# Spreading filter rows by DMA from SBUF to SBUF in an FFT-filter and max-out kernel

## Chip, cores, metric

One core of one Trainium2 chip. The metric is the device time of one execution in microseconds (us), the median of the runs of one session. All runs compared here are in the fast state or, where there was only one run, of unknown state; no slow run is used. Ratios are the mean time of one kernel's runs over the mean time of the other's in the same rounds, so not quite the ratio of the medians that are quoted.

## The reference

```python
X = np.fft.rfft(x, axis=1)                    # x: 8 x 3072 x 256
Y = X * (filt_r + 1j * filt_i)[None]          # filter: 1537 x 256
y = np.fft.irfft(Y, n=3072, axis=1).reshape(24576, 256)
out = np.maximum(y @ w1, y @ w2) @ w_out      # w1, w2: 256 x 1024; w_out: 1024 x 256
```

## The kernel before

Each batch goes through four transform stages: S1 (matrix C1, result `at`, written to HBM as `ad`, read back as `bt`), S2 (matrix U, result `px`; VectorE multiplies it by the filter rows F to `pq`), S3 (matrices VP and VQ, result `zt`, written as `zd`, read back as `zr`) and S4 (G1, result `y`). Then come 48 tiles of the second half: `ph` = y against w1 - w2, a relu to `gt`, and `po` = gt against w_out. A tile has eight steps of about 1 us, and the transform of the next batches is planned into these steps. Batch 0 goes through a special *opening* before the first `ph`.

F must hold the filter rows in a spread order of partitions (groups of 12 rows, every eighth source row). TensorE makes it with selection matrices from `Fs`, which has the rows as they lie in HBM, and ScalarE or VectorE evict the result:

```python
    def expand_f(g, ri, E, sp=0):
        ...
        for b in range(2):
            for c in range(2):
                m = 4 * b + c
                TE.matmul(pf[b][64 * c:64 * c + 32], Sel[:, m], fs[:, 2 * g:2 * g + 2], start=True, stop=True)
                ...                                   # and the mirrored rows, 32 partitions on
        evac(E, f_, p_...)                            # to F[:, ri, :, 2 * g:2 * g + 2]
```

The opening in the order of its program (cut); `first_s2` makes px and pq of one group g of rows:

```python
    V.memset(F0[:, :, :, 0:1], 0.0)
    load_f0()                       # 12 small DMAs on SyncE
    patch_f0()                      # 2 more, into rows that one of the 12 wrote
    first_s1(5, S, 2)
    expand_f(6, 0, V)
    ...
    expand_f(1, 1, S)
    expand_f(7, 0, S)
    pend = []
    for n, g in enumerate((1, 2, 3, 4, 5, 0, 6, 7)):
        pend.append(first_s2(g, n in (0, 1, 2, 4, 6)))
        if n < 6:
            first_t1(order[n + 2], V)
        ...
        if n < 6:
            expand_f((0, 3, 4, 5, 6, 7)[n], 1, S)
        ...
        if n > 1:
            first_s3(*pend.pop(0))
```

The plan of the first batches:

```python
    plan(6, f1_read, 1)                               # bt of batch 1
    plan_f2(1, spaced(17, 1.9, 9), 28, 34)            # S2/S3 of batch 1; zr in halves at 28 and 34
    plan_x(2, (5, 7, 8, 10, 11, 13), 6)               # load and fold x of batch 2
    plan(36, f1_read, 2)
    plan_x(3, spaced(24, 3, 6))
```

## Time and profile before

| | before |
|---|---|
| time, median of 2 | 527.7 us (527.67 to 527.74) |
| span in the profile | 523.8 us |
| TensorE busy | 504.0 us (96%) |
| pq of step n=3 starts | 29.92 us |
| last pq of the opening ends | 43.94 us |
| first `ph` starts | 48.24 us |
| from there to the end | 475.6 us |

The span splits at the first `ph`: ahead of it other engines pace TensorE, after it TensorE is nearly dense. The profiled execution took 525.53 us, some 2 us less than the median.

### The profile page before, as it was taken

How to read it: one execution, taken by the hardware profiler on the slowest of the kernel's cores; microseconds unless marked ns; L12 is line 12 of the kernel's file. 1: busy time of each engine (PE TensorE's matmuls, PEld its weight loads, DVE VectorE, ACT ScalarE, POOL GpSimd, SP SyncE). 2: the span in 40 equal slices, each digit the busy share in tenths (PEclk: the TensorE clock that was granted, in tenths of full speed). 3: DMA queues.
4: the chain of work that ended last, by engine and by line, in shares of the span. 5: the costliest groups of instructions: out<-in, count | busy, mean ns of one | idle time of the engine just before them, and what ended most of it. 6: DMA issues, size and time to landing. Idle time of an engine off the chain costs nothing.

```text
span 523.8 us, 12526 instructions
## 1 busy us (share of the span) xinstructions
PE 504.0 (96%) x5204; PEld 346.5 (66%) x5282; DVE 322.4 (62%) x437; ACT 336.9 (64%) x597; POOL 148.0 (28%) x168
## 2 busy tenths in 40 slices
PE   8988989999999999999999999999999999999997
PEld 3556655666667766676666666676667666677775
DVE  8986567435773476437783588537783588544432
ACT  6786658746885588756675577647675556645542
POOL 6683118264027204530066002720000000000000
PEclk9999999999999999999999999999999999999999
DMA  7990699997798969796798769894467936341212
GB/s 143 280 204 23 176 199 320 334 204 177 232 247 241 208 195 300 229 200 185 219 266 201 182 179 241 266 202 139 143 172 157 176 111 150 100 125 41 82 62 100
DMA packets 74093, 97.03 MB, mean 185 GB/s; under 512 B 5106, under 2 KB 49780, under 8 KB 73044
## 3 DMA queue, kind: packets, MB, share of 16 engines
q1 hardware_dynamic: 63012, 63.72, 52.6%
q0 software_dynamic: 11024, 32.51, 20.1%
q8 instruction: 41, 0.67, 0.6%
q14 instruction: 16, 0.13, 0.1%
HBM read 54.79 MB, written 47.19 MB: 195 GB/s over the span
## 4 chain that ended last, share of the span: by engine, by line
PE 76%; issue 1%; DVE 1%; ACT 0%
PE po L621 30%; PE ph L596 26%; PE po L616 7%; PE pz L447 4%; PE py L580 3%; PE px L469 2%; PE pa L410 2%; DVE pq L474 0%; ACT at L413 0%; DVE ot L623 0%
## 5 line engine op out<-in xcount | busy, mean ns | idle before, releaser
L601 ACT ACTIVATE gt<-ph 128x512 bf16<-128x512 f32 x308 | 182.1, 603 | 125.5 <-PE ph L596 124.0
L621 PE MATMUL po<-Wo,gt 128*128 128x256 bf16 x1536 | 229.8, 273 | 3.4
L621 PEld LDWEIGHTS <-gt 128*128 128x128 bf16 x1536 | 150.2, 98 | 57.6
L474 DVE TENSOR_TENSOR pq<-px,F 120x1024 bf16<-120x1024 f32 x112 | 131.7, 1219 | 32.6 <-PE px L469 32.4
L623 DVE COPY ot<-po 128x512 f32<-128x512 f32 x96 | 66.2, 690 | 103.9 <-PE po L621 102.3
L628 POOL DMA_DIRECT2D out_dram<-ot x47 | 25.8, 548 | 311.0 <-DVE ot L623 298.8
L402 POOL TENSOR_TENSOR xd<-xf 128x512 bf16<-128x512 f32 x72 | 89.1, 1268 | 47.2 <-DMA xf<-in_x_dram 46.2
L596 PEld LDWEIGHTS <-Wd 128*128 128x128 bf16 x768 | 70.8, 98 | 21.2 <-issue 12.6
L451 ACT ACTIVATE zt<-pz 112x512 bf16<-112x512 f32 x112 | 61.0, 602 | 19.5 <-PE pz L447 16.4
L599 DVE TENSOR_SCALAR gt<-ph 128x512 bf16<-128x512 f32 x76 | 52.2, 687 | 29.4 <-PE ph L596 22.0
L413 ACT ACTIVATE at<-pa 128x512 bf16<-128x512 f32 x72 | 39.2, 596 | 15.6 <-PE pa L410 15.4
L580 PE MATMUL py<-G,zr 128*128 128x128 bf16 x384 | 30.1, 219 | 1.9 <-ACT zr L514 0.7
L447 PE MATMUL pz<-pq,VP 56*64 56x256 bf16 x448 | 29.4, 271 | 1.1 <-DVE pq L474 0.8
L580 PEld LDWEIGHTS <-zr 128*128 128x128 bf16 x384 | 25.3, 98 | 5.1 <-issue 3.6
L447 PE MATMUL pz<-pq,VQ 56*64 56x256 bf16 x448 | 28.6, 268 | 0.0
L469 PE MATMUL px<-bt,U 48*64 48x256 bf16 x448 | 23.5, 274 | 1.0 <-DMA bt<-ad 1.0
L469 PEld LDWEIGHTS <-U 48*64 48x64 bf16 x448 | 11.6, 106 | 9.2 <-issue 6.0
L447 PEld LDWEIGHTS <-VP 56*64 56x64 bf16 x448 | 14.1, 105 | 3.7 <-issue 2.4
L530 DVE TENSOR_TENSOR pq<-px,F 120x1024 bf16<-120x1024 f32 x11 | 13.2, 1222 | 3.5 <-ACT F L514 1.9
L410 PE MATMUL pa<-xd,C 64*64 64x512 bf16 x144 | 15.2, 400 | 0.0
L514 ACT ACTIVATE F<-pf 128x1024 bf16<-128x1024 f32 x10 | 10.1, 1032 | 6.7 <-PE pf L134 6.7
L447 PEld LDWEIGHTS <-VQ 56*64 56x64 bf16 x448 | 13.9, 106 | 0.0
(387 smaller groups left out, 591.2 us busy)
## 6 DMA issues: line engine op xcount, KB each, us to landing
out_dram<-ot POOLq DMA_DIRECT2D x47, 512.0 KB, 5.1
xf<-in_x_dram SPq DMA_DIRECT2D x72, 256.0 KB
ad<-at SPq DMA_DIRECT2D x42, 256.0 KB
bt<-ad SPq DMA_DIRECT2D x56, 192.0 KB
zd<-zt SPq DMA_DIRECT2D x56, 192.0 KB
zr<-zd SPq DMA_DIRECT2D x14, 768.0 KB
xb<-in_x_dram POOLq DMA_DIRECT2D x12, 256.0 KB, 10.6
wf<-in_moe_w_dram POOLq DMA_DIRECT2D x2, 1024.0 KB, 10.3
```

The lines of the kernel that those rows point to most:

```text
L402: G.tensor_tensor(xb[b, c][:, i], xf[:, 0], xf[:, 1], op)
L413: S.activation(at[:, 2 * m:2 * m + 2], pa[m], AF.Copy)
L447: TE.matmul(pz[c][64 * k:64 * k + 64, i], W[64 * c:64 * c + 56, 2 * g + i, k], pq[k][64 * c:64 * c + 56, ri, i], start=(ri == 0), stop=(ri ...
L451: S.activation(zt[0:ROWS, c, o:o + 2], pz[c][0:ROWS], AF.Copy)
L469: TE.matmul(px[k][64 * c:64 * c + 64, i], U[64 * k:64 * k + 48, 4 * g + 2 * i + c], bt_[64 * k:64 * k + 48, t_], start=True, stop=True)
L474: V.tensor_tensor(pq[k][0:FROWS], px[k][0:FROWS].rearrange("p (o i) d -> p o i d", o=1).to_broadcast([FROWS, 2, 2, D]), F[0:FROWS, :, k, 2 ...
L580: TE.matmul(py[:, n], zr[b][:, 4 * i + n, 128 * dc:128 * dc + 128], G1, start=True, stop=True)
L596: TE.matmul(ph, Wd[:, dc, 128 * j:128 * j + 128], y_[:, dc].rearrange("p a b -> p (a b)"), start=(dc == 0), stop=(dc == 1))
L599: V.tensor_scalar(gt[tt][:, j], ph, 0.0, None, OP.max)
L601: S.activation(gt[tt][:, j], ph, AF.Relu)
L621: TE.matmul(p_, g_[:, jj, 128 * n:128 * n + 128], Wo[:, jj], start=False, stop=(jj == 7))
L623: V.tensor_copy(ot[tt][:, n - 1:n + 1], po[tt])
```

## The change

The intent: take evictions off ScalarE and products off TensorE in the opening by letting the idle SyncE queue spread the later filter rows (groups 6 and 7 of the real half, 4 to 7 of the imaginary half) by 32 DMAs from Fs to F; move x loads of batch 2 into the time where the DMA engines are idle; give S2/S3 of batch 1 twenty steps instead of seventeen. The core of the diff:

```diff
+    def spread_f(ri, g0):
+        n = 16 - 2 * g0
+        for b in range(2):
+            for c in range(2):
+                m = 4 * b + c
+                for q in range(2):
+                    p0 = 64 * c + 12 * q
+                    nc.sync.dma_start(out=F[p0:p0 + J, ri, b, 2 * g0:16], in_=Fs[ri][m:m + 89:8, 2 * g0:16])
+                    nc.sync.dma_start(out=F[p0 + 32:p0 + 32 + J, ri, b, 2 * g0:16],
+                                      in_=Fs[ri][7 - m:96 - m:8, n:0:-1])
 ...
+    clear_f(0, 6, G)            # zeros under the copied rows, on GpSimd
 ...
+    clear_f(1, 4, S)            # and on ScalarE
 ...
-    expand_f(6, 0, V)
+    expand_f(1, 1, S)
     first_t1(1, V)
     first_t1(2, V)
-    expand_f(1, 1, S)
-    expand_f(7, 0, S)
+    spread_f(1, 4)
+    spread_f(0, 6)
+    expand_f(2, 1, S)
 ...
-            first_t1(order[n + 2], V)
+            first_t1(order[n + 2], (V, S)[n > 2])
 ...                             # 4 expansions less in the loop, Wd(0) from GpSimd to VectorE at n=3
+    f1(1, 0, S)                 # S1 of batch 1: four parts in the tail of the opening
+    f1(1, 1, V)
+    for c in (3, 4, 5):
+        load_p(2, c)            # half of x of batch 2
 ...
-    s4(0)
-    f1(1, 0, V)
-    f1(1, 1, S)
+    first_s4()                  # S4 of tile 0 in halves
+    f1(1, 2, V)
+    f1(1, 3, S)
 ...
-    plan(6, f1_read, 1)
-    plan_f2(1, spaced(17, 1.9, 9), 28, 34)
-    plan_x(2, (5, 7, 8, 10, 11, 13), 6)
+    plan(5, f1_read, 1)
+    plan_f2(1, spaced(15, 2.4, 9), 28, 36)
+    for c in range(3):
+        plan(6 + c, load_p, 2, c)
+        plan(7 + 2 * c, fold_x, 2, 3 + c)
+        plan(15 + 2 * c, fold_x, 2, c)
```

More of the change, by code (lines that the diff above doesn't have):

```diff
@@ L143, in expand_f, with clear_f @@
             evac(E, f_, p_.rearrange("p b u d -> p b (u d)"))
+    def spread_f(ri, g0):
[8 more added lines that the diff above has]
+                                      in_=Fs[ri][7 - m:96 - m:8, n:0:-1])
+    def clear_f(ri, g0, E):
+        f_ = F[:, ri, :, 2 * g0:16].rearrange("p b u d -> p b (u d)").bitcast(FP32)
+        if E is S:
+            S.activation(f_, zero.rearrange("p (a b) -> p a b", a=1).to_broadcast([128, 2, (16 - 2 * g0) * D // 2]), AF.Copy)
+        else:
+            E.memset(f_, 0.0)
     F0 = zpool.tile([64, 2, 2, D], FP32, tag="zt", name="F0")
@@ L338, in spin, with prep_wd @@
             TE.matmul(pd, Sp, Sp.rearrange("p (o x) -> p o x", o=1).to_broadcast([128, 4, 128]), start=True, stop=True)
-    def prep_wd(k, w1f, w2f):
-        G.tensor_tensor(Wd[:, k], w1f[:, k], w2f[:, k], OP.subtract)
+    def prep_wd(k, E, w1f, w2f):
+        E.tensor_tensor(Wd[:, k], w1f[:, k], w2f[:, k], OP.subtract)
     def load_wo():
@@ L386, in load_p @@
     def load_p(b, c):
-        if c == 0:
+        if b not in big and c < 3:
             big[b] = late.tile([128, 3, 2, 2 * D], FP32, tag="l0", name="xf")
@@ L404, in f1_half @@
     def f1_half(b, c):
-        if c == 0:
+        if b not in ad:
             ad[b] = dram.tile([128, N2, D], BF16, tag="ad", name="ad")
@@ L463, in gen_f2 @@
             if b + 1 < B and j in units:
-                f1_half(b + 1, units.index(j))
+                f1_half(b + 1, (3, 4, 5, 0, 1, 2)[units.index(j)] if b == 1 else units.index(j))
             px = [ps.tile([128, 2, D], FP32, tag="ps", name="px") for _ in range(2)]
@@ L586, in s4, with first_s4 @@
         yt[tt] = y_
+    def first_s4():
+        y_ = ypool.tile([128, 2, 4, 128], BF16, tag="yt")
+        for h in range(2):
+            for dc in range(2):
+                py = ps.tile([128, 2, 128], FP32, tag="ps", name="py")
+                for n in range(2):
+                    TE.matmul(py[:, n], zr[0][:, 2 * h + n, 128 * dc:128 * dc + 128], G1, start=True, stop=True)
+                o = y_[:, dc, 2 * h:2 * h + 2]
+                if dc == 0:
+                    S.activation(o, py, AF.Copy, scale=1.0 / 1536.0)
+                else:
+                    V.tensor_scalar(o, py, 1.0 / 1536.0, None, OP.mult)
+        yt[0] = y_
     gt = {}
@@ L683 @@
         if n < 6:
-            first_t1(order[n + 2], V)
+            first_t1(order[n + 2], (V, S)[n > 2])
         if n == 0:
             tables_pe()
-            expand_f(2, 1, S)
-        if n < 6:
-            expand_f((0, 3, 4, 5, 6, 7)[n], 1, S)
+        if n < 2:
+            expand_f((3, 0)[n], 1, S)
         if n < 2:
@@ L693 @@
             fix_f()
-        if n in (1, 3):
-            tables_q(n // 2, S)
-        if n in (4, 6):
-            prep_wd(n // 2 - 2, *wf)
+        if n in (1, 2):
+            tables_q(n - 1, S)
+        if n == 3:
+            prep_wd(0, V, *wf)
+        if n == 6:
+            prep_wd(1, G, *wf)
         if n in (4, 5):
@@ L748 @@
         plan(j - 1, first_t2, j, V)
-    for c in range(2, 12):
-        plan(int(0.6 * (c - 1)), f1, 1, c, (S, V)[c % 2])
-    plan(6, f1_read, 1)
-    plan_f2(1, spaced(17, 1.9, 9), 28, 34)
-    plan_x(2, (5, 7, 8, 10, 11, 13), 6)
+    for c in range(4, 12):
+        plan(int(0.6 * (c - 3)), f1, 1, c, (S, V)[c % 2])
+    plan(5, f1_read, 1)
[4 more added lines that the diff above has]
+        plan(15 + 2 * c, fold_x, 2, c)
     plan(36, f1_read, 2)
@@ L771, in in_f2 @@
     def in_f2(step):
-        return 0 <= step < 6 or 17 <= step < 35 or 60 <= step < 82 or 104 <= step < 130
+        return 0 <= step < 6 or 15 <= step < 36 or 60 <= step < 82 or 104 <= step < 130
     for tt in range(6 * B + 1):
```

## The prediction

> **What bounds the kernel now.** I read the page first, then the busy time by stretches, then the opening's timelines of VectorE and of the SyncE queue, then the DMA view of short stretches.
>
> ```profile
> PE 504.0 (96%) x5204; PEld 346.5 (66%) x5282; DVE 322.4 (62%) x437; ACT 336.9 (64%) x597; POOL 148.0 (28%) x168
> ...
> DMA  7990699997798969796798769894467936341212
> ...
> PE 76%; issue 1%; DVE 1%; ACT 0%
> ```
>
> TensorE sets the time: it is busy 96% of the span and is nearly the whole of the chain that ended last. No change of evictions or loads can help where it is already dense, so I looked for the stretches where it isn't (columns: PE, PEld, DVE, ACT, POOL busy, PE clock, DMA share, GB/s).
>
> ```profile
> 0.00:48.24 48.24, 41.79 (x678) 24.29 (x682) 40.05 (x95) 35.70 (x53) 33.46 (x49) 1.00 0.83 171
> 48.24:116.00 67.76, 63.68 (x617) 42.89 (x626) 40.22 (x50) 45.52 (x84) 27.46 (x25) 1.00 0.93 237
> 116.00:500.00 384.00, 378.56 (x3757) 264.44 (x3819) 234.25 (x283) 247.91 (x448) 85.52 (x91) 1.00 0.72 184
> ```
>
> 48.24 us is where the first product of the second half (ph) starts. From 116 us on TensorE lacks 5.4 us of 384, all of it outside the change. From 48 to 116 us it lacks 4.1 us. The opening is the rest: 41.79 us busy there include 7.16 us of the 25 idle-filling matmuls at the start, so it is held by chains through the other engines. In its second half VectorE paces it:
>
> ```profile
> 29.92 2.36 DVE L530 TENSOR_TENSOR pq<-px,F 120x1024 bf16<-120x1024 f32 x2 [0.51 <-ACT F L514]
> ...
> 33.40 1.22 DVE L530 TENSOR_TENSOR pq<-px,F 120x1024 bf16<-120x1024 f32 x1 [0.53 <-ACT VQ L514]
> ...
> 41.58 2.36 DVE L530 TENSOR_TENSOR pq<-px,F 120x1024 bf16<-120x1024 f32 x2 [0.70 <-issue]
> ```
>
> These multiply S2's result by the filter rows F. Step n=3 (rows g=4) starts at 29.92 us, the last step ends at 43.94, and the first ph follows 4.3 us later. VectorE waits about half a us per step for ScalarE's copies of F, VQ and the like.
>
> **Where the DMA stands.** The new copies go out on SyncE behind the small loads of F0, so their present timing matters most:
>
> ```profile
> 18.59 2.31 SPq L154 DMA_DIRECT2D F<-in_filt_r_dram  x6
> 20.94 5.21 SPq L154 DMA_DIRECT2D F<-in_filt_i_dram  x6
> 27.77 0.24 SPq L157 DMA_DIRECT2D F<-in_filt_i_dram  x1
> 28.06 0.25 SPq L158 DMA_DIRECT2D F<-in_filt_r_dram  x1
> ```
>
> The first eight leave one after the other (298 to 435 ns each); the ninth leaves only at 23.85 us, and the wait view names the landing of a filter-row DMA. Nine waits for one: this program keeps eight of a queue in flight. The first one needed 23.85 - 18.59 = 5.3 us to land, the second patch (the fourteenth DMA) leaves at 28.06. The DMA views of 18 to 22 us and of 22 to 26 us show why:
>
> ```profile
> q0 software_dynamic: 513, 1.27, 104.8%
> ```
>
> ```profile
> q0 software_dynamic: 339, 1.20, 91.8%
> q1 hardware_dynamic: 205, 0.15, 13.3%
> ```
>
> In the first stretch SyncE's queue (q1) got not one packet; in the second about as many per engine as the GpSimd loads (q0). Those loads fill the engines until about 39 us.
>
> [...]
>
> **The change, part by part.**
>
> *Six expansions fewer.* Of 16 expansions of F (8 matmuls, about 0.44 us of TensorE each, and an eviction) groups 6 and 7 of the real and 4 to 7 of the imaginary half go. TensorE saves 6 x 0.44 = 2.6 us, ScalarE 5 evictions of 0.92 us pitch = 4.6 us, VectorE two of 0.6 = 1.2 us. Added: a clear of 2048 elements on ScalarE, by the like clear of At (1.89 us), which fits in its idle 2.17 us before 9.78; one on GpSimd, at most some 1 us (a guess), ahead of load issues that wait for landings anyway (1.8 us before the one at 9.36). Both cost nothing on the path.
>
> *Work moved to balance.* Three copies of bt (0.6 us pitch on VectorE, 1.0 on ScalarE) go to ScalarE at n=3 to 5, and half of Wd (2.34 us on GpSimd, as a tensor product of 1024 elements like pq some 1.15 on VectorE) to VectorE. VectorE gains 0.6 us, ScalarE 1.6.
>
> *32 copies from SBUF to SBUF.* Half move 12 rows as 12 long pieces, half as 12 x 8 (or 12 x 4) pieces of 512 B. The first 16 (imaginary, g 4 to 7) are 16 x 12 x 4 KB = 0.79 MB, the other 16 half that. They follow the patch at 28.06 us. Issue alone at 0.35 us: 28.4 + 16 x 0.35 = 34; plus some 2 us to land, **36 us** is the earliest for the row groups that n=3 needs at 29.92. With eight in flight, a landing of 3 to 5 us in the full queue and turns with q0 it is more. Per engine a 4 KB piece of q0 at the 209 GB/s of 30 to 38 us takes 4 KB / (209/16) = 0.31 us; the copies, from the 47 ns that a 490 B packet took in 64 to 68 us, about 0.4 us for eight small pieces and 0.15 for a long one (estimates). Eight pairs: 8 x (2 x 0.31 + 0.55) = 9.4 us, with start and landing 28.4 + 9.4 + 2 = **40 us**. I choose **38**.
>
> From there VectorE has left: eight pq (two at n=3, 5 and 7, one at n=4 and 6, where GpSimd makes the other) at a pitch of 1.15 us (two took 2.36) = 9.2, Wd 1.15, two w2T copies 1.2: 11.55 us. The end of pq goes to 38 + 11.6 = 49.6, against 43.94: **+5.6 us**. GpSimd and ScalarE work in parallel below that. The second 16 copies are needed some 7 us after the first and should be there.
>
> *End of the opening.* Four parts of batch 1's S1 run in TensorE's gaps of 44 to 48 us instead of one before the first ph: 3 x 0.22 = 0.65 us; S4 split in halves shortens the chain by perhaps 0.3: **-0.9 us**.
>
> *First batches.* Between 67 and 72 us S2 of batch 1 waits 0.37 + 0.64 us for bt and 0.84 us for VectorE; at 89 to 91 us 0.22 and 0.64 more, at 113 us 0.46; some slow matmuls beside these. Half of x of batch 2 now comes in the idle 39 to 48 us, bt is read before the other half, and 20 steps instead of 17 ease VectorE and ScalarE. Of 4.1 us I take **-2.8**.
>
> Sum: 527.7 + 5.6 - 0.9 - 2.8 = **529.6**, rounded to 529.5 us.
>
> **Rivals.** *(A) The copies come in time*: then ScalarE's freed 4.6 - 3.0 - 0 = 1.6 us and VectorE's 0.6 shorten steps 3 to 7 by 2 to 3 us, and the time is 527.7 - 2.5 - 0.9 - 2.8 = 521.5. For it: somebody tuned which groups are copied and moved work from exactly those steps. Against: the queue's 28.06 us. *(B) Full turns with the GpSimd loads*, and each small piece taking its own turn: first group at 44 us, opening +11.6, time 527.7 + 11.6 - 3.7 = 535.6; [...] *(C) The loop doesn't gain*, because bt's reads of 512 B pieces are what is late (about 160 GB/s in 64 to 72 us), not the x loads beside them: then 529.6 + 2 = 531.5.
>
> **Range and chances.** A and B bound the likely outcomes: 521 to 536. To be over 2% faster needs 10.6 us; all idle of the first batches and 6 us of opening together hardly give it: 0.03. Over 2% slower needs first groups after 47 us: 0.04. The rest, 0.93, lies within 2%; inside it I hold faster and slower about even, leaning to slower.
>
> **What would show it.** In the changed profile: the first spread copy leaves SyncE at about 28.4 us and the sixteenth between 34 and 38; VectorE's pq of n=3 waits for a DMA of F, not for ScalarE, and starts at 36 to 41 us instead of 29.9; first ph near 53 us; PEclk may dip in the third to fourth slice. From the first ph to the end the time is 2 to 4 us shorter, with no wait of px for bt. Wrong if pq of n=3 starts before 33 us (then the copies left earlier or landed in about 2 us), or if some later wait for F's second copies, or for xb, ends the opening.

## The result, and the profile after

548.5 us (547.16 and 549.84) against 527.7: ratio 1.0394, 95% interval 1.0285 to 1.0503. The change is slower by 3.9%, outside the predicted range.

The page of the changed kernel, TensorE's clock in 40 slices and the chain that ended last by engine:

```profile
PEclk9985789998999999999999999999999999999999
...
PE 79%; DMA 9%; SPq 4%; DVE 4%; ACT 1%; issue 1%; POOL 0%; POOLq 0%; DVEq 0%; ACTq 0%
```

Before, the clock row was 9 throughout and the chain had neither DMA nor SPq, the queue that SyncE issues from. Now the end hangs on 9% of DMA and 4% of *issuing*. The SyncE queue's timeline after (start, duration, line; L152 and L153 are the two copies of `spread_f`):

```profile
29.31 0.24 SPq L175 DMA_DIRECT2D F<-in_filt_i_dram  x1
29.59 0.25 SPq L176 DMA_DIRECT2D F<-in_filt_r_dram  x1
30.02 0.86 SPq L152 DMA_DIRECT2D F<-Fs  x1
30.99 0.88 SPq L153 DMA_DIRECT2D F<-Fs  x1
...
36.02 0.82 SPq L153 DMA_DIRECT2D F<-Fs  x1
...
44.25 0.82 SPq L153 DMA_DIRECT2D F<-Fs  x1
...
57.73 0.82 SPq L153 DMA_DIRECT2D F<-Fs  x1
```

The first copy leaves at 30.02 us, the eighth at 36.02, the sixteenth at 44.25, the last at 57.73. One copy takes 0.74 to 0.96 us to issue, where the F0 loads of the same profile took 0.27 to 0.44. Two of the copies (the twelfth and the fourteenth) also waited up to 1.0 us until an earlier one had landed: the fourteenth left at 42.60, when the sixth had (34.38 + 8.21 us). While the second sixteen go out, the DMA engines have almost nothing to do. The DMA view of 46 to 58 us has for SyncE's queue (packets, MB, share of the 16 engines' time):

```profile
q1 hardware_dynamic: 602, 0.35, 11.2%
```

VectorE's products pq in the opening after, which answer to those at 29.92, 33.40 and 41.58 us before:

```profile
43.42 1.22 DVE L549 TENSOR_TENSOR pq<-px,F 120x1024 bf16<-120x1024 f32 x1 [12.46 <-DMA F<-Fs]
47.12 1.22 DVE L549 TENSOR_TENSOR pq<-px,F 120x1024 bf16<-120x1024 f32 x1 [2.48 <-DMA F<-Fs]
...
60.22 1.23 DVE L549 TENSOR_TENSOR pq<-px,F 120x1024 bf16<-120x1024 f32 x1 [0.50 <-PE pz L567]
```

Step n=3 waits 12.46 us for its first product (rows b=0, in the first eight copies) and 2.48 for its second (b=1, the next eight). The last products can't start before the last copy, whose issue ended at 58.55 and which landed at 59.9 us; for VectorE's last one the timeline names only the wait that it took to be the last, one for TensorE, but the chain that ended last runs through the copies (four of its pieces: start, duration, what):

```profile
34.38 8.21 DMA F<-Fs
...
57.73 2.17 DMA F<-Fs
...
60.24 2.13 POOL pq L549
...
62.42 0.52 PE pz L567 x28
```

The piece of 8.21 us is the sixth copy, from its issue to its landing. The last product on this chain isn't VectorE's but GpSimd's, for step n=6 (rows b=1): it had waited 10.8 us for the copies and ended at 62.4 us, while GpSimd's last product before had ended at 42.2, ahead of VectorE's. The first `ph` starts at 67.93 us.

TensorE's clock was granted at 0.54 between 46 and 58.6 us and at 0.82 from there to 67.93 (0.50 in each whole microsecond from 65 to 71): the matmuls that prepare the first tile run partly at half speed. At tile 6 the clock fell after a wait of 4.36 us (below). In the opening it fell between 37 and 38 us (1.00 in the microsecond before, 0.50 in the one after), though TensorE had been busy for 1.94 us of 33 to 37 us, by matmuls whose ends the profile models. It fell again between 64 and 65 (1.00 before, 0.50 after), where its longest pause in the 4 us before was 1.79 us (until 62.42). What makes the clock fall isn't shown.

The second loss is at tile 6, whose S4 needs zr of batch 1. TensorE's timeline after:

```profile
127.90 0.59 PE L629 MATMUL ph<-y__2011,Wd 128*128 128x512 bf16 x2
...
133.40 1.01 PE L599 MATMUL py<-G,zr 128*128 128x128 bf16 x8 [4.36 <-DMA zr<-zd]
134.67 1.11 PE L629 MATMUL ph<-y__2144,Wd 128*128 128x512 bf16 x2 [0.26 <-ACT y__2144 L602]
```

A wait of 4.36 us for zr, and then ph takes 1.11 us instead of 0.59: the clock has dropped again (0.98 from 127 to 133 us, 0.50 from 133 to 139).

| | before | after | difference |
|---|---|---|---|
| pq of n=3 starts | 29.92 | 43.42 | +13.5 |
| from there to the end of the last pq | 14.0 | 18.0 | +4.0 |
| from there to the first ph | 4.3 | 6.5 | +2.2 |
| from there to the end | 475.6 | 479.9 | +4.3 |
| span | 523.8 | 547.8 | +24.0 |

Here "last pq" is VectorE's. The profiled executions took 525.53 and 549.84 us, one faster and one slower than its kernel's median, so the 24.0 us are 3.2 more than the 20.8 between the medians; in which rows these lie isn't known.

### The profile page after: what moved, and what is told of

Same layout as the page of the kernel before. It is cut to its first block, busy times and chain, and to the rows that moved or that the text cites.

```text
span 547.8 us, 12572 instructions
## 1 busy us (share of the span) xinstructions
PE 513.6 (94%) x5234; PEld 350.0 (64%) x5234; DVE 323.5 (59%) x434; ACT 337.1 (62%) x597; POOL 146.5 (27%) x168
## 4 chain that ended last, share of the span: by engine, by line
PE 79%; DMA 9%; SPq 4%; DVE 4%; ACT 1%; issue 1%; POOL 0%; POOLq 0%; DVEq 0%; ACTq 0%
PE ph L629 30%; PE po L654 29%; PE po L649 7%; PE pz L466 4%; PE py L599 3%; DMA zd<-zt 3%; PE px L488 3%; PE pa L429 2%; DMA F<-Fs 2%; SPq L152 2%; SPq L153 2%; DMA zr<-zd 1%; DMA F<-in_filt_i_dram 1%; DVE F L141 1%; DMA ad<-at 1%
## 5 line engine op out<-in xcount | busy, mean ns | idle before, releaser
L488 PE MATMUL px<-bt,U 48*64 48x256 bf16 x448 | 22.6, 274 | 0.5 <-DMA bt<-ad 0.5
L549 POOL TENSOR_TENSOR pq<-xs,F 120x1024 bf16<-120x1024 f32 x5 | 10.7, 2137 | 23.9 <-ACT M L533 11.0
L540 PE MATMUL px<-bt,U 48*64 48x256 bf16 x64 | 4.5, 313 | 10.2 <-DVE pq L549 10.0
```

The costliest lines, as they stand in the source:

```text
L488: TE.matmul(px[k][64 * c:64 * c + 64, i], U[64 * k:64 * k + 48, 4 * g + 2 * i + c], bt_[64 * k:64 * k + 48, t_], start=True, stop=True)
```

## The experiments

Twelve kernels ran, each beside the kernel before on the same chip. That one's medians were 527.7 to 528.4 us in the four sessions.

### The two halves of the change

**e1_no_spread**: the changed kernel with the opening of the kernel before.

```diff
-    clear_f(0, 6, G)
-    clear_f(1, 4, S)
-    spread_f(1, 4)
-    spread_f(0, 6)
+    ...   # all 16 expansions, their order and engines as before
```

> The opening as before, the rest of the change kept (half of x of batch 2 in the opening, S1 parts and split S4 in the tail, 20-step S2/S3). Theory (the 32 copies on SyncE's queue cost the opening its 20 us): the first ph starts at 47 to 48.5 us. If the wait of 4.4 us for zr at tile 6 is the schedule's own, the rest takes about 478 us and the time is 526 to 530; if that wait only followed from the late opening, the rest takes 472 to 474 us and the time is 521 to 524. Rival (other opening edits cost the 20 us): the first ph is still after 60 us.

Measured: 526.67 us, ratio 0.9988 (0.9941 to 1.0035): the same as before. The first ph is at 48.27 us. Two lines of TensorE's wait view from 48 to 140 us (us in total, times, longest):

```profile
PE px L487 <- DMA bt<-ad: 2.0, 2, 1.1
PE py L598 <- DMA zr<-zd: 1.9, 1, 1.9
```

So the loss is in the opening's copies and what goes with them, and the rest of the change brings nothing as it stands. S2 starts two steps earlier, but bt isn't there: the wait for it doubled from 1.0 to 2.0 us (1.09 and 0.91), and TensorE ran slowly for some 3 us after it (68 to 71.5 us: a pair of ph took 1.06 us at 69.44 and 0.59 at 63.92; the clock was 0.91 in 60 to 70 us and 0.92 in 70 to 80). And there is a wait of 1.9 us for zr that the kernel before doesn't have.

**e2_only_spread**: the complement. Copies, clears and moved work in the opening; tail and loop as before.

```diff
+    ...   # against the kernel before: spread_f, clear_f, the rebalanced opening
     # tail, plan_f2(1, spaced(17, 1.9, 9), 28, 34), plan_x(2, (5, 7, 8, 10, 11, 13), 6) as before
```

> The complement: only the copies, the clears and the work moved with them in the opening, the tail and the loop as before. Theory: the first ph starts at 66 to 69 us, the rest takes 475 to 477 us as in the kernel before, so 543 to 547 us. Rival (the loss comes from x of batch 2 loaded early, competing for the DMA engines): the first ph before 55 us and a time under 535.

Measured: 550.15 us, ratio 1.0423 (1.0385 to 1.0461), first ph at 68.28 us. The early x loads are not needed for the loss. The time was 3 us over the expected range: in this late opening even the old loop waited 2.4 us for bt and 0.8 for zr. No run kept the moved work without the copies, so that the copies and not the moved work cost the time rests on the waits for `DMA F<-Fs` and on e3.

### Issue or transfer

**e3_short_copies**: every copy cut to one row of 512 B per partition, the result wrong.

```diff
-    nc.sync.dma_start(out=F[p0:p0 + J, ri, b, 2 * g0:16], in_=Fs[ri][m:m + 89:8, 2 * g0:16])
+    nc.sync.dma_start(out=F[p0:p0 + J, ri, b, 15:16], in_=Fs[ri][m:m + 89:8, 15:16])
     # the mirrored copy likewise
```

> The changed kernel with each of the 32 copies cut to one row of 512 B per partition (a wrong result on purpose). Theory (SyncE needs about 0.8 us to issue a copy, whatever it moves): the copies still take 26 to 28 us to issue and the first ph is at 65 to 68 us. Rival (the bytes and small pieces, sharing the engines with the GpSimd loads, are what is slow): the 32 copies leave in 11 us at 0.35 us each and the first ph is at 52 to 56 us.

Measured (one run): 544.47 us. SyncE's queue:

```profile
29.75 0.86 SPq L152 DMA_DIRECT2D F<-Fs  x1
30.66 0.73 SPq L153 DMA_DIRECT2D F<-Fs  x1
31.43 0.71 SPq L152 DMA_DIRECT2D F<-Fs  x1
...
53.79 0.71 SPq L153 DMA_DIRECT2D F<-Fs  x1
```

A copy of an eighth or a quarter of the bytes still takes 0.71 us to issue, and the 32 take 24.8 us (29.75 to 54.50). In this run the cost goes with the instruction, not with the bytes. The first ph came at 62.10 us, before the expected 65 to 68: with one row only group 7 waits for a copy, so steps 3 to 6 went ahead, and the issue itself is some 4 us shorter (24.8 us against 28.5). 62.10 - 48.24 = 13.9 us of loss therefore remain when hardly any bytes are moved.

**e5_dma_forms**: the kernel before with test DMAs at the head of SyncE's queue, 512 B a row.

```diff
+    for i in range(3):
+        p0 = (0, 12, 32)[i]
+        Q.dma_start(out=tdst[p0:p0 + 12, 0], in_=tsrc[i:i + 89:8])              # L194
+        Q.dma_start(out=tdst[64 + p0:64 + p0 + 12, 0], in_=tsrc[p0:p0 + 12])    # L195
+        Q.dma_start(out=tdst[112:128, 0], in_=tsrc[16 * i:16 * i + 16])         # L196
+        Q.dma_start(out=tdst[48:64, 0], in_=tsrc[i:i + 121:8])                  # L197
+        Q.dma_start(out=tdr[12 * i:12 * i + 12], in_=tsrc[12 * i:12 * i + 12])  # L198, to HBM
+        Q.dma_start(out=tdst[p0:p0 + 12, 0].bitcast(FP32), in_=filt_r[12 * i:12 * i + 12, 0:128])  # L199, from HBM
+    # and two each of 64 rows (L201), 128 rows (L202), 1 row (L203)
```

> The kernel before with 24 small test DMAs at the head of SyncE's queue, rows of 512 B: SBUF to SBUF with 12 rows every eighth partition, 12 neighbouring rows, 16 neighbouring rows, 16 rows every eighth partition, 64 and 128 rows, 1 row; 12 rows SBUF to HBM; 12 rows HBM to SBUF. What it tells: which property makes an issue cost 0.71 to 0.82 us instead of the 0.30 us of the F0 loads. If SBUF at both ends: every SBUF to SBUF form with 12 or 16 rows takes 0.7 us, HBM forms 0.3. If the count of 12: the 16-row forms take 0.35 us. If the partition step of 8: the neighbouring rows take 0.35 us.

Measured, by line of the source (issue in ns, minimum/median/maximum):

```profile
L194 SPq DMA_DIRECT2D tdst<-tsrc x3: 806/815/916, 1.2 to 11.2; - x3
L195 SPq DMA_DIRECT2D tdst<-tsrc x3: 736/740/746, 2.1 to 12.1; - x3
L196 SPq DMA_DIRECT2D tdst<-tsrc x3: 559/559/588, 2.9 to 14.4; - x3
L197 SPq DMA_DIRECT2D tdst<-tsrc x3: 536/537/892, 3.5 to 15.1; - x3
L198 SPq DMA_DIRECT2D tdr<-tsrc x3: 537/549/553, 4.5 to 15.7; - x3
L199 SPq DMA_DIRECT2D tdst<-in_filt_r_dram x3: 304/357/501, 5.1 to 16.4; - x3
L202 SPq DMA_DIRECT2D tdst<-tsrc x2: 477/495/513, 26.8 to 39.8; - x2
L203 SPq DMA_DIRECT2D tdst<-tsrc x2: 535/540/544, 32.7 to 41.6; - x2
```

None of the three single causes holds alone. HBM to SBUF with 12 rows took 357 ns (median), SBUF to HBM with 12 rows 549, SBUF to SBUF with 12 rows 740 to 815, with 16 rows 537 to 559, with 64 rows 501, with 128 rows 495, with 1 row 540. In this run the two ends and the count of 12 both cost; the partition step of 8 costs little (815 against 740 with 12 rows, 537 against 559 with 16). Why isn't shown. (This run's own 543.86 us, from one execution of unknown state, says nothing of the question: the test DMAs stand ahead of the kernel's loads.)

**e9_two_queues**: half of the copies on GpSimd's queue.

```diff
-    spread_f(1, 4)
-    spread_f(0, 6)
+    spread_f(1, 4, 0, nc.sync)          # rows b=0 only
+    spread_f(0, 6, 0, nc.sync)
 ...
         if n == 2:
+            spread_f(1, 4, 1, G)        # rows b=1
             fix_f()
+            spread_f(0, 6, 1, G)
```

> The changed kernel with half of the copies (those of b=1) issued by GpSimd in its idle time around 32 to 47 us, the other half by SyncE; same bytes, same engines. Theory (one queue's issue time is the bound): SyncE's 16 copies leave between 30 and 43.5 us, the last of F is there by 47 to 50 us instead of 60, the first ph is at 57 to 62 us instead of 68, time 538 to 543. Rival (the 16 engines are the bound once the copies run): the last F row still lands at 57 us or later, the first ph stays within 2 us of 68.

Measured: 546.67 us, ratio 1.0353 (1.0314 to 1.0391), first ph at 64.33 us. Neither side was right in full, and the time missed the theory's 538 to 543. All copies had been issued by 50.50 us instead of 58.55, and the first ph came 3.6 us earlier, where the theory wanted 6 to 11. On GpSimd's queue a copy took 0.51 to 0.64 us to issue, but seven of the first eight there waited 0.49 to 1.66 us each for the landing of that queue's own loads, and the eighth left at 42.97. But pq of n=3 didn't start earlier:

```profile
44.40 1.23 DVE L549 TENSOR_TENSOR pq<-px,F 120x1024 bf16<-120x1024 f32 x1 [14.58 <-DMA F<-Fs]
```

SyncE's first eight copies had been issued by 35.8 us and the product waited until 44.40. In the changed kernel, too, the eighth copy was out at 36.84 us and the product waited until 43.42. At that time the loads of GpSimd's queue still fill the engines (its share is 93.5% in 34 to 38 us of the changed kernel and 33.1% in 38 to 42). So by the traces the full engines are a bound of their own for the first eight copies, beside the issue; for the last sixteen it is the issue alone, at 11% engine share. A faster issue of the first eight wasn't tried. From pq of n=3 to VectorE's last pq this run still took 15.6 us (44.40 to 60.03), 2.4 less than the changed kernel: no product waited for a copy after 47.1 us, but VectorE waited 2.4 us for px, and TensorE's matmuls ran slowly until 56 us (eight for pm took 1.83 us at 54.73 and 1.05 at 57.55).

**e8_clear_act**: the GpSimd clear moved to ScalarE.

```diff
-    clear_f(0, 6, G)
+    clear_f(0, 6, S)            # next to clear_f(1, 4, S)
```

> The changed kernel with the GpSimd clear of 1024 elements of F moved to ScalarE. Theory (the GpSimd clear holds up VectorE at 5 to 8 us): VectorE's pauses of about 1 us at 5.4 and 7.1 us go, F0's clear comes at 18.5 us instead of 20.2, the first copy leaves at 28 to 29 us instead of 30.0; the first ph 1 to 1.5 us earlier at most. Rival (those pauses have another cause): unchanged.

Measured: 545.63 us, ratio 1.0330 (1.0301 to 1.0359). The changed kernel was at 1.0394, so their intervals overlap and only the trace separates them. VectorE in the changed kernel, then in this run:

```profile
5.38 1.22 DVE L274 TENSOR_SCALAR off<-off 128x2 f32<-128x2 f32 x1
...
7.12 0.95 DVE L281 TENSOR_SCALAR kb<-kb,col 128x24 f32<-128x24 f32 x1
```

```profile
5.38 0.31 DVE L273 TENSOR_SCALAR off<-off 128x2 f32<-128x2 f32 x1
```

Both pauses are gone (the second instruction takes 0.26 us instead of 0.95), F0 is cleared at 18.58 us instead of 20.16, the first copy leaves at 28.85 instead of 30.02, and the first ph is at 66.90, 1.0 us earlier. The size is loose: with the GpSimd clear in place the first copy left between 29.02 and 30.02 us (five traces), and e4's first ph came at 67.13. Of the five kernels with the GpSimd clear whose traces I compared, four show both pauses (the changed kernel, e2, e3, e4) and e9 only the first; of five without it (before, e1, e6, e8, e11) none shows either. The clear is recorded from 7.06 to 8.04 us: the second pause lies in it (7.12 to 8.07), the first before it (5.38 to 6.60); the profile's spans on GpSimd are rough. By what the clear holds VectorE up isn't shown.

### The loop

**e4_old_f2**: the changed kernel with the old plan of S2/S3.

```diff
-    plan_f2(1, spaced(15, 2.4, 9), 28, 36)
+    plan_f2(1, spaced(17, 1.9, 9), 28, 34)
```

> The changed kernel with S2/S3 of batch 1 planned as before (steps 17, gap 1.9, zr read at 34). Theory (the later last S3 and zr read make tile 6 wait): the 4.4 us wait for zr goes, TensorE's clock doesn't drop there, and the time is 541 to 544. Rival (the reads queue behind x loads and older reads in any case): a wait of 3 us or more stays and the time is 547 to 549.

Measured: 545.97 us, ratio 1.0343 (1.0288 to 1.0398). That lies between the two expected ranges, and its interval overlaps that of the changed kernel, so only the traces, one of each, separate them. The wait for zr fell from 4.4 to 2.5 us, the clock row no longer dips there (the second and third pair of ph after the wait take 0.43 us each in the chain that ended last, in the changed kernel 0.85). The wait didn't go: the plan is part of its cause, not all.

**e6_no_spread_old_f2**: e1 with the same edit as e4.

> As the run without copies, and S2/S3 of batch 1 planned as before (steps 17, gap 1.9, zr read at 34). Theory (starting S2 two steps earlier only moved the wait onto bt, and ending S3 two steps later moved one onto zr): the waits of px for bt (2.0 us) and of py for zr (1.9 us) go or fall under 1 us together, time 1.5 to 3 us under the run without copies, thus 523 to 525 and 0.5 to 1% under the kernel before. Rival (the chain write of ad, read of bt, write of zd, read of zr is bound by the DMA engines, whatever the plan): 2 us or more of these waits stay and the time is within 0.3% of the kernel before.

Measured: 524.93 us, ratio 0.9952 (0.9928 to 0.9977). The wait for bt fell to 0.4 us, that for zr stayed at 1.8: the time is where the theory had it, the 2.2 us of waits are where the rival had them. In the chain of this run the wait is made of a zd write that takes 8.05 us to land and a zr read that takes 7.37.

**e7_x3_later**: e6 with x of batch 3 ten steps later.

```diff
-    plan_x(3, spaced(24, 3, 6))
+    plan_x(3, spaced(34, 3, 6), 9)
```

> The last one, and x of batch 3 loaded ten steps later (from step 34 instead of 24), so that it doesn't share the DMA engines with the writes of zd and the read of zr. If the wait for zr comes from these loads: zd lands in 2 to 4 us instead of 6, no wait of py for zr, 0.5 to 1.5 us faster than without this. If not: the same time.

Measured: 532.63 us, ratio 1.0092 (1.0069 to 1.0114), 0.9% longer. The wait for zr did fall to 0.6 us, but another took its place:

```profile
PE pz L465 <- DVE pq L492: 6.4, 3, 4.8
```

The chain view shows how: a fold of x on GpSimd waited for its load until 121.8 us, the stores of the output queue on GpSimd behind the folds, one store landed at 131.5, the buffer `ot` came free, VectorE's copy into it ran, and only then the pq that TensorE was waiting for.

**e10_x3_early**: e6 with x of batch 3 at steps 18 to 27.

```diff
-    plan_x(3, spaced(24, 3, 6))
+    for c, s_ in zip((3, 4, 5, 0, 1, 2), (18, 20, 22, 23, 25, 27)):
+        plan(s_, load_p, 3, c)
+    ...                                 # folds at 36, 39, ... as before
```

> No copies, old S2/S3 plan, and x of batch 3 loaded at steps 18 to 27 instead of 24 to 39, folded when it was before. Theory (x loads in front of the last zd write and the zr read make tile 6 wait): the wait of py for zr (1.8 us) falls under 0.5 us, time 0.5 to 2 us under the run with x as before (524.9): 523 to 524.5. Rival (earlier loads only delay bt and the other zd writes): a new wait of 1 us or more before step 30, no gain.

Measured: 527.71 us, ratio 1.0002 (0.9977 to 1.0028). The wait for zr grew to 2.8 us. Its last zd write began to move at 98.80 us, in e6 at 95.99 (by the chains); what held it up isn't settled.

**e11_x3_gap**: e6 with a gap in the x loads around the last zd writes and zr reads.

```diff
-    plan(36, f1_read, 2)
-    plan_x(3, spaced(24, 3, 6))
+    plan(40, f1_read, 2)
+    for c, s_ in zip((3, 4, 5, 0, 1, 2), (24, 27, 35, 36, 37, 38)):
+        plan(s_, load_p, 3, c)
+    for c, s_ in zip((3, 4, 5, 0, 1, 2), (38, 40, 50, 52, 54, 56)):
+        plan(s_, fold_x, 3, c)
```

> As that, but with two of the six x parts at steps 24 and 27, none until the zr read of step 34, the rest at 35 to 38 and the read of bt for batch 2 at 40. Theory: no wait for zr and no late folds, 523 to 524.5. Against: the folds of 50 to 56 wait for their loads as in the run with x ten steps later, hold up the stores of the output behind them, and cost 1 to 5 us.

Measured: 522.47 us (522.26 to 522.89), ratio 0.9908 (0.9881 to 0.9935), the fastest version here. TensorE's waits from 45 to 140 us, all that the view lists:

```profile
PE pz L465 <- DVE pq L492: 0.8, 1, 0.8
PE py L612 <- ACT zr L532: 0.7, 1, 0.7
PE ph L628 <- ACT y__2166 L601: 0.5, 1, 0.5
PE ph L628 <- ACT y__1152 L615: 0.3, 1, 0.3
PE pt L580 <- DVE Zt L530: 0.2, 1, 0.2
```

No DMA is left among them. The edit moves three things (the x loads, their folds and the read of bt for batch 2); which of them counts wasn't separated.

**e12_before_x3_gap**: the kernel before with nothing but this plan for x of batch 3.

> The kernel before with nothing but the plan for x of batch 3 and the read of bt for batch 2 of the last run. It splits the 0.9% of that run. If the gain comes from this plan alone: 522 to 523.5. If it comes from the kept parts of the change (half of x of batch 2 in the opening, S1 parts and split S4 in the tail), which only couldn't show as long as tile 6 waited for zr: 526.5 to 528, and the waits of px for bt (1.0 us) and of pz and py for VectorE (1.4 us) between 67 and 92 us are still there.

Measured: 525.98 us, ratio 0.9953 (0.9928 to 0.9978). It lies just under the range that gives the kept parts all the gain, and it is still slower than e11: about half of the 0.9% comes with this plan on the kernel before and the other half, less surely since the two intervals overlap a little, with the kept parts of the change. As expected the waits for bt (0.9 us) and the 0.8 us of pz for VectorE are still there. One caution: its profiled span, 523.8 us, is that of the kernel before, so the 0.5% rests on the timed runs alone.

## Why the prediction was wrong

**Right**: TensorE as the bound after the first ph; the SyncE queue as what would be late, and the order behind F0 (first copy predicted at 28.4 us, measured 30.02); pq of n=3 waiting for a DMA of F; a dip of the clock (to 0.50 in 38 to 46 us), which no trace had shown by then; full engines behind the GpSimd loads (93.5% in 34 to 38 us). The prediction also named the sign that came true: it would be wrong if "some later wait for F's second copies" ended the opening.

**The step that failed** is the cost of the 32 copies, in two of its terms. The first is "Issue alone at 0.35 us". That size was taken from HBM loads on the same queue. The copies took 0.74 to 0.96 us; e3 shows that the bytes are not the cause (0.71 to 0.92 us with an eighth or a quarter of them), and e5 that the form is (medians of 740 and 815 ns from SBUF to SBUF with 12 rows, 537 and 559 with 16, 357 from HBM with 12). The second is "some 2 us to land", with the 9.4 us for the eight pairs. The last copy, with the engines at 11%, did land 2.17 us after the start of its issue; but the issue of the eighth copy ended at 36.84 us and pq of n=3 could start only at 43.42, 6.6 us later, while SyncE's queue had 17.1% of the engines' time (34 to 38 us) beside 93.5% for the GpSimd loads. Against the predicted terms:

| term | predicted | measured | difference |
|---|---|---|---|
| pq of n=3 starts | 38 us | 43.42 us | +5.4 |
| from there to the end of pq | 11.6 us | 18.0 us | +6.4 |
| tail to the first ph, against before | -0.9 us | +2.2 us | +3.1 |
| loop, against before | -2.8 us | +4.3 us | +7.1 |

Of the first row's 5.4 us about 4.6 are the landing (an estimate: with the predicted 2 us, 36.84 + 2 = 38.8 us would have been the start). The row flatters the prediction: its 38 us stood for all sixteen copies of the imaginary half, and the sixteenth let pq of n=3 go on only at 47.12.

The second row hides a step that failed in kind: "The second 16 copies are needed some 7 us after the first and should be there." They weren't. From 45.17 to 58.55 us SyncE did nothing but issue them, and the last pq followed the last landing at 59.9 us. With that the opening had a second bound that the rivals lacked; e3 shows that 13.9 us of loss remain with hardly any bytes. But without that bound the row would not have been 11.6 us: in e9, where no product waited for a copy after 47.1 us, it is 15.6, with slow matmuls on TensorE until 56 us. Rival B had the first groups at 44 us, nearly the measured 43.4, yet its time was 535.6, because it took the rest of the opening as VectorE's 11.6 us.

The third row: 0.9 us of it is GpSimd's product, which ended at 62.36 us and VectorE's last at 61.45; "GpSimd and ScalarE work in parallel below that" failed here. S4 in halves and the S1 parts shorten nothing that is seen when the opening is on time either (first ph at 48.27 in e1 against 48.24), and in the changed kernel the clock was at 0.50 for the last 3 us of the tail. The prediction's terms hold no time for a lower clock; it showed at the tail, where TensorE is on the path (eight matmuls for py took 1.01 us, before the change 0.61), and in e9's wait for px (eight took 0.64 us at 54.16, 0.41 at 57.21). How many of these us the clock cost by itself was not measured.

The fourth row: "bt is read before the other half, and 20 steps instead of 17 ease VectorE and ScalarE" was an argument about waits that were there, and not about those that would come. Starting S2 at step 15 ran into bt (e1: 2.0 us), ending S3 and reading zr later ran into tile 6 (1.9 us in e1, 4.4 in the changed kernel), so e1 gained nothing. e6 and e11 show that some of the predicted gain was there: with the old plan and the x loads held away from the zd and zr transfers, the loop gives about 1%. In the changed kernel the 4.4 us came with a half-speed stretch after it (0.50 from 133 to 139 us).

Smaller slips: "Both cost nothing on the path" was wrong for the GpSimd clear, with which VectorE paused by 0.9 and 0.7 us and F0 was cleared at 20.16 us instead of 18.58 (e8). The 0.15 us for a long piece doesn't follow from 47 ns for 490 B, which gives 0.39; with that the eight pairs take 11.3 us and n=3 starts at about 41.7 (estimates). The turns behind the 9.4 us and rival B (a row of a copy per engine, a q0 piece of 4 KB before each) were an estimate: the views give 205 packets of q1 against 339 of q0 in 22 to 26 us, which are not "about as many", 1.8 KB per q0 packet in 34 to 38 us (0.81 MB in 447), and no count per engine. 529.6 + 2 is 531.6, not 531.5.

Why 12 rows are dearer to issue than 16 (e5: 740 and 815 ns against 537 and 559) is open. That the time of the x loads matters for the zr wait is shown by e7 and e10 against e6; e11 moved the bt read too. Why e10 lost is open.

## What to carry to other kernels

In this case work moved to a queue that looked idle had a price per instruction, 0.74 to 0.96 us. Count the DMAs, take the issue time from a DMA of the same form (both ends, row count) and not from one that merely uses the same queue (0.27 to 0.44 us here), and multiply; here the issuing took 28.5 us (30.02 to 58.55), more than all the pq of the opening had taken before (21.58 to 43.94). When a wait goes away in a chain of writes and reads through HBM, look at the next transfer of the chain and at what else is queued beside it before you count the gain.
